# Band attention into a mixture of experts on one core: how w1 is prepared in the second pass, and three moved steps

## Chip, core and metric

One core of one Trainium2 chip runs the whole program. The metric is the device time of one execution in microseconds, the median over several runs. Times inside an execution come from the hardware profiler, counted from the span's start.

## What is computed

Attention over a band, then a mixture of experts on its result. Everything is float32.

```python
# q, k, v: (4, 8, 576, 64); window 32; heads 4 to 7 with dilation 4
scores = scale * q @ k.T, masked to the band
attn   = softmax(scores)
x      = (attn @ v) as (2304, 512)
# w1: (4, 512, 1024), w2: (4, 1024, 512), p: (2304, 4) from domain_probs
for e in range(4):
    out += p[:, e:e+1] * (relu(x @ w1[e]) @ w2[e])
```

## The kernel before

**Units and blocks.** The 4 experts are cut into 16 units of 256 hidden columns (u), the 2304 rows of x into 3 blocks of 768 (m). Each float32 operand is split into a high half, rounded to the type that TensorE multiplies (ScalarE's copy), and a low half, the rest (a subtraction on VectorE or GpSimd); a product is three matmuls. Most products are done by Strassen's scheme: seven products of quarter matrices in place of eight, with sums of quarters as operands. The operands of w1 are A11, A12, A22 and the sums S1 to S4 of its quarters, those of x B11, B21, B22 and T1 to T4, those of w2 the seven parts P1 to P7.

**First pass** (to about 277 us of the span). Units 0 to 11 meet block 0 while attention still runs. The generator `experts` yields one piece of TensorE work after another; the main loop takes one piece, calls `flush`, then lets the current round of attention (`pairs_of_steps`) go on by one yield, then a step of the queue of preparations. `split` makes a high half at once and puts the subtraction into `held` when something is holding; `flush` issues what is held. `mm1_b` is the second part of a unit's seven products: it asks for each part of x by `need_x` (which calls `need`, which calls `flush` first and last), multiplies, and lets VectorE add two results (s at L638, u at L643). In `mm1_b` "room" lets `room` make a preparation of x with the low half held. A round of attention ends with the copies `s_out` (ScalarE, L517) of the previous steps' output and with `s_norm` (GpSimd, L404) of the new ones. Each prepared w1 operand of units 2 to 11 is stored in HBM (`keep_w1`).

**Second pass** (from 277 us). 18 groups, each a pair of units on a block, in the order of `groups`. The loop over n runs the first products (`m1`, 14 pieces) of group n beside the second products (`m2`, P1, P5, P6, P3, P7, P2, P4) of group n-1; iteration n has seven steps b, each with two pieces of `m1`, one of `m2` and a call of `background(b)`. After every piece of `m1` the SP queue gets the load of that operand for the next unit (L833), which waits until TensorE has read the old one. In front of and behind the products stand ScalarE's copies out of PSUM (L884, L888, L890, L896) and its high halves (L904), VectorE's sums (L886, L892, L894, L932), low halves (L911, L916) and weighted sums into `acc` (L690).

`background(b)` issues two kinds of preparation. `w2_parts` makes the seven parts of w2 for the next pair: high half on ScalarE (L992), low half on GpSimd (L993), sums on GpSimd (L997, L1000, L1005, L1010). It starts when a new pair begins (`n in begins`: 2, 4, 6, 8, 10, 12, 13, 15, 17) with step 1 and goes on into the first two steps of the next iteration. `w1_again` does the same for w1 of units 12 to 15, 0 and 1, whose operands were not kept: it loads the rows of w1 into one tile (L1017), then for each of seven operands makes the sum if there is one (GpSimd, L1030), the high half (ScalarE, L1033) and the low half (GpSimd, L1034) into one tile `again`, and stores it (SP, L1036). Each of these is one call; `background` makes three calls a step, two where a pair begins, from iteration 1 on:

```python
            t = pools["late"].tile([128, 2, 2, 128], F32R, tag="again", name="again")
            nc.scalar.activation(out=t[:, 0], in_=src, func=AF.Copy)
            tt(out=t[:, 1], in0=src, in1=t[:, 0].bitcast(F32), op=ALU.subtract)
            yield
            nc.sync.dma_start(
...
                for _ in range(3 - (n in begins) if n else 0):
                    if again and next(again[0], 0) == 0:
                        again.pop(0)
```

All engines work through their own instructions in the order written here; a scheduler moves nothing.

Of the kernel before, what the change touches and what calls it, by code (L numbers as in the profile page):

```python
# [8 lines left out]
F32 = mybir.dt.float32  # L9
F32R = mybir.dt.float32r  # L10
# [38 lines left out]
def kernel(  # L49
# [231 lines left out]
    def attention(ap, xrp, pa, steps):  # L281
# [120 lines left out]
        def s_norm(n, gs):  # L402
            sm, rc = st[n]
            nc.gpsimd.tensor_tensor(  # L404
                out=sm, in0=sm, in1=rc.unsqueeze(2).to_broadcast([128, 2 * GS, KB]),
                op=ALU.mult,
            )
            st[n] = sm
# [93 lines left out]
        def s_out(n, gs, engines=None):  # L502
            po = st.pop(n)
            for k, (b, p, gi) in enumerate(gs):
                x = x_raw(b)[:, p, :]
                src = po[k][:, :GW]
                if p < NP // 2:
                    nt = GW // DILATION
                    dst = x.rearrange("q (r t) -> q r t", r=DILATION)
                    dst = dst[:, :, gi * nt:(gi + 1) * nt]  # L510
                    src = src.rearrange("q (t r) -> q r t", r=DILATION)
                else:
                    dst = x[:, gi * GW:(gi + 1) * GW]
                if engines and engines[k] == "v":
                    nc.vector.tensor_copy(out=dst, in_=src)
                else:
                    nc.scalar.activation(out=dst, in_=src, func=AF.Copy)  # L517
# [18 lines left out]
        def pairs_of_steps(new, old, begun, loaded):  # L536

            for m in old:
                s_tr(m, steps[m])
            if old:  # L540
                yield
            if new and not begun:
                for stage in (s_qk, s_max):
                    for m in new:
                        stage(m, steps[m])
                yield
            for stage in (s_sub, s_exp):
                for m in new:
                    stage(m, steps[m])
                    yield  # L550
            if not begun:
                loaded(len(new), 0)
                yield
            s_sums([(m, steps[m]) for m in new])
            for m in old:
                s_av(m, steps[m], True)
            for m in old[:1]:
                s_out(m, steps[m])
            yield
            for m in old[1:]:  # L560
                s_out(m, steps[m])
            if old:
                loaded(0, len(old))
                yield
            for m in new:
                s_norm(m, steps[m])
                yield

        return chunk, load_masks, load_qk, load_v, stages, at_first, pairs_of_steps

# [53 lines left out]
    def mm1_b(k):  # L624
        u, m = k
        x, u2, s5 = st.pop(k), tmp("u2"), tmp("s5")
        need_x(m, ("T2",))
        product(x, u, "S2", m, "T2", False)
        nc.scalar.activation(out=u2, in_=x, func=AF.Copy)
        yield "room"  # L630
        y = bank("x")
        need_x(m, ("T1",))
        product(y, u, "S1", m, "T1", True)
        nc.scalar.activation(out=s5, in_=y, func=AF.Copy)
        yield "room"
        need_x(m, ("T3",))
        product(x, u, "S3", m, "T3", False)
        nc.vector.tensor_tensor(out=s5, in0=x, in1=s5, op=ALU.add)  # L638
        yield
        need_x(m, ("B22",))  # L640
        product(y, u, "S4", m, "B22", False)
        h_hi(k, "22", s5)
        nc.vector.tensor_tensor(out=u2, in0=y, in1=u2, op=ALU.add)  # L643
        h_lo(k, "22", s5)
        h_out(k, "12", u2)
        yield "full"
        need_x(m, ("T4",))
        product(x, u, "A22", m, "T4", False)
        h_out(k, "21", x)
        yield "full"  # L650
# [364 lines left out]
    def w1_again(u, r):  # L1015

        nc.sync.dma_start(out=r, in_=w1_rows(u))  # L1017
        kept[u] = dram.tile([NO, 128, 2, FU], F32, name=f"w1_{u}")
        yield
        a11, a12 = r[:, 0:2, 0:128], r[:, 2:4, 0:128]  # L1020
        a21, a22 = r[:, 0:2, 128:256], r[:, 2:4, 128:256]
        tt = nc.gpsimd.tensor_tensor
        for n, src, one, two, op in (
            ("A11", a11, None, None, None), ("A12", a12, None, None, None),
            ("A22", a22, None, None, None), ("S1", a22, a21, a22, ALU.add),
            ("S3", a21, a11, a21, ALU.subtract), ("S2", a11, a22, a11, ALU.subtract),
            ("S4", a12, a12, a11, ALU.subtract),
        ):
            if op is not None:
                tt(out=src, in0=one, in1=two, op=op)  # L1030
                yield
            t = pools["late"].tile([128, 2, 2, 128], F32R, tag="again", name="again")
            nc.scalar.activation(out=t[:, 0], in_=src, func=AF.Copy)  # L1033
            tt(out=t[:, 1], in0=src, in1=t[:, 0].bitcast(F32), op=ALU.subtract)  # L1034
            yield
            nc.sync.dma_start(  # L1036
                out=kept[u][KEPT.index(n)].rearrange("p s f -> p (s f)"),
                in_=t.bitcast(F32).rearrange("p s c f -> p (s c f)"),
            )
            yield  # L1040

    def second_pass(tiles):

# [32 lines left out]
        for n in range(len(groups) + 1):  # L1076
# [18 lines left out]
                    first_over()  # L1095

            def background(b):
                if n == 0 and b < 5 or n and n in begins and b > 0 or n - 1 in begins and b < 2:
                    while w2_steps and next(w2_steps[0], 0) == 0:
                        w2_steps.pop(0)  # L1100
                if n + 1 in begins:
                    run = begins.index(n + 1)
                    if b in (2, 3):
                        spare = n in begins and (
                            raw_again.rearrange("p c f -> p (c f)").rearrange(
                                "p (c d) -> p c d", c=2
                            ), pools["other"],
                        )
                        if spare:
                            assert not again  # L1110
                        fetch_w2_half(runs2[run][0][b - 2], spare and spare[b - 2] or None)
                    elif b == 6:
                        w2_steps.append(w2_parts())
                for _ in range(3 - (n in begins) if n else 0):
                    if again and next(again[0], 0) == 0:
                        again.pop(0)
                if n == BACK + 1:
                    away_x(PRODUCTS[b][1], True)
                if n == BACK + 2 and b == 4:
                    acc_t[0] = acc_t[1]  # L1120
                    nc.sync.dma_start(
                        out=acc_t[0], in_=away["acc"].rearrange("a p d -> p a d")
                    )
# [540 lines left out]
```

## Time and profile before

| | us |
|---|---|
| median of 3 runs | 832.32 (830.87 to 834.38) |
| the profiled execution, its own time | 834.22 |
| span of the profiled execution | 832.2 |
| TensorE busy | 796.6 |
| VectorE busy | 611.0 |
| ScalarE busy | 361.5 |
| GpSimd busy | 406.6 |
| mean granted TensorE clock | 0.989 of full speed |

The span is the time from the first to the last instruction of one execution; the rest of its time lies around it. Busy time counts instructions at work, without waits. A wait is told as idle time of an engine just before an instruction, with what ended it.

### The profile page before, as it was taken

The numbers are of one execution on the slowest core, as the hardware profiler recorded it, in microseconds if no ns is written. First come the engines' busy times: TensorE is split into PE (matmuls) and PEld (weight loads), VectorE is DVE, ScalarE is ACT, GpSimd is POOL, SyncE is SP. The second block draws the span as 40 slices with busy tenths as digits, with TensorE's granted clock in tenths as the row PEclk, the third lists the DMA queues.
The fourth block names the chain that finished last, engine by engine and source line by source line (L and its number), as shares of the span: only waits on it lengthen the run. The fifth ranks groups of instructions, "written<-read, shape, count | busy, mean of one in ns | idle before, by whom it ended". The sixth has DMA issues, their size and how long they took to land.

```text
span 832.2 us, 18128 instructions
## 1 busy us (share of the span) xinstructions
PE 796.6 (96%) x6998; PEld 751.9 (90%) x6998; DVE 611.0 (73%) x1267; ACT 361.5 (43%) x723; POOL 406.6 (49%) x388
## 2 busy tenths in 40 slices
PE   7999999999999989899898999999999999999997
PEld 4778888888888879889898999999999999999997
DVE  6787666666686576667756687886977988788697
ACT  5455454544555344433533443443433454244341
POOL 5646796877696334725642661520511553052051
PEclk9999999999999999989998999999999999999998
DMA  8768668875668666465465566444454546965612
GB/s 243 213 185 246 217 214 258 287 264 188 215 218 280 203 212 202 152 203 184 158 208 171 155 201 212 125 147 151 124 171 125 178 127 221 380 226 176 214 38 77
DMA packets 108561, 161.60 MB, mean 194 GB/s; under 512 B 8873, under 2 KB 57513, under 8 KB 108475
## 3 DMA queue, kind: packets, MB, share of 16 engines
q1 hardware_dynamic: 107771, 159.88, 60.2%
q8 instruction: 56, 0.92, 0.5%
q10 hardware_dynamic: 704, 0.56, 0.2%
q14 instruction: 30, 0.25, 0.1%
HBM read 119.25 MB, written 41.16 MB: 193 GB/s over the span
## 4 chain that ended last, share of the span: by engine, by line
PE 71%; DVE 8%; POOL 6%; DMA 6%; ACT 5%; issue 3%; SPq 0%; DVEq 0%; POOLq 0%; ACTq 0%
PE m1x L577 21%; PE x L950 15%; PE m1y L577 11%; PE y L950 10%; PE m L709 10%; DMA w<-again 3%; DVE acc L690 2%; DMA r<-w 2%; POOL w_P L993 2%; PE po L435 2%; PE sc L346 1%; POOL again L1034 1%; DVE xr L257 1%; POOL sm L404 1%; DMA qk_s<-kT 1%
## 5 line engine op out<-in xcount | busy, mean ns | idle before, releaser
L993 POOL TENSOR_TENSOR w_P<-r,w_P 128x512 fp32r<-128x512 f32 x70 | 98.8, 1411 | 246.1 <-ACT w_P L992 127.5
L690 DVE SCALAR_TENSOR_TENSOR acc<-x,pn,acc 128x256 f32<-128x256 f32 x198 | 83.1, 473 | 8.8 <-PE x L950 8.7
L932 DVE SCALAR_TENSOR_TENSOR g<-g 128x768 f32<-128x768 f32 x72 | 88.6, 1230 | 0.6
L1034 POOL TENSOR_TENSOR again<-r,again 128x256 fp32r<-128x256 f32 x42 | 36.7, 874 | 87.5 <-ACT again L1033 87.5
L577 PE MATMUL m1x<-xh_B,s_A 128*128 128x384 f32 x288 | 74.0, 338 | 3.6 <-ACT g L884 3.6
L690 DVE SCALAR_TENSOR_TENSOR acc<-y,pn,acc 128x256 f32<-128x256 f32 x156 | 65.5, 473 | 11.2 <-PE y L950 10.7
L950 PE MATMUL y<-w_P,h0h 128*128 128x256 f32 x432 | 69.8, 284 | 1.5 <-ACT h0h L904 1.5
L950 PE MATMUL x<-w_P,xh_T 128*128 128x256 f32 x432 | 71.1, 288 | 0.0
L690 DVE SCALAR_TENSOR_TENSOR acc<-m,pn,acc 128x512 f32<-128x512 f32 x66 | 49.1, 748 | 29.5 <-PE m L709 29.5
L992 ACT ACTIVATE w_P<-r 128x512 fp32r<-128x512 f32 x70 | 43.9, 627 | 50.9 <-POOL r L1010 22.4
L950 PEld LDWEIGHTS y<-w_P,h0h 128*128 128x128 f32 x432 | 61.6, 191 | 2.1 <-ACT h0h L904 2.1
L950 PEld LDWEIGHTS x<-w_P,xh_T 128*128 128x128 f32 x432 | 63.1, 195 | 0.0
L577 PE MATMUL m1y<-xh_B,s_S 128*128 128x384 f32 x208 | 54.8, 345 | 7.4 <-ACT g L888 7.4
L577 PE MATMUL m1x<-xh_T,s_S 128*128 128x384 f32 x224 | 58.1, 341 | 3.0 <-ACT g L890 2.9
L709 PE MATMUL m<-w2h,hh 128*128 128x512 f32 x144 | 58.7, 408 | 1.2 <-DVE acc L690 1.1
L1033 ACT ACTIVATE again<-r 128x256 fp32r<-128x256 f32 x42 | 17.5, 416 | 96.9 <-DMA w<-again 57.9
L916 DVE TENSOR_TENSOR h0l<-g,h0h 128x768 fp32r<-128x768 f32 x36 | 38.6, 1072 | 25.9 <-ACT h0h L904 25.8
L709 PE MATMUL m<-w2l,hh 128*128 128x512 f32 x144 | 56.5, 393 | 0.0
L577 PEld LDWEIGHTS m1x<-xh_B,s_A 128*128 128x128 f32 x288 | 51.1, 188 | 4.5 <-ACT g L884 4.5
L904 ACT ACTIVATE h0h<-g 128x768 fp32r<-128x768 f32 x36 | 30.3, 841 | 56.7 <-DVE g L932 56.7
L911 DVE SCALAR_TENSOR_TENSOR h1l<-g,h1h 128x768 fp32r<-128x768 f32 x18 | 24.3, 1350 | 33.8 <-ACT h1h L904 33.8
L577 PE MATMUL m1x<-xl_B,s_A 128*128 128x384 f32 x144 | 48.4, 336 | 0.0
(215 smaller groups left out, 2274.9 us busy)
## 6 DMA issues: line engine op xcount, KB each, us to landing
s_S<-w SPq DMA_DIRECT2D x144, 256.0 KB, 2.8
s_A<-w SPq DMA_DIRECT2D x108, 256.0 KB, 2.8
r<-w SPq DMA_DIRECT2D x49, 512.0 KB, 4.1
w<-again SPq DMA_DIRECT2D x42, 256.0 KB, 2.0
v_s<-vw SPq DMA_DIRECT2D x48, 192.0 KB, 5.1
w<-g2h SPq DMA_DIRECT2D x10, 512.0 KB, 4.9
w<-g2l SPq DMA_DIRECT2D x10, 512.0 KB, 5.8
k_s<-kT SPq DMA_DIRECT2D x21, 224.0 KB, 5.2
```

The costliest lines, as they stand in the source:

```text
L577: nc.tensor.matmul(bank, w[:, k], x[:, k], start=(first and k == 0 and n == 0), stop=(last and k == 1 and n == len(parts) - 1), skip_group ...
L690: nc.vector.scalar_tensor_tensor(out=acc, in0=po, scalar=pn[:, tt, e:e + 1], in1=acc, op0=ALU.mult, op1=ALU.add,)
L709: nc.tensor.matmul(po, h, w, start=(n == 0 and x == 0), stop=(n == 3))
L904: nc.scalar.activation(out=h_places[n][0], in_=source(g, n), func=AF.Relu if n in RAW else AF.Copy)
L911: nc.vector.scalar_tensor_tensor(out=l, in0=source(g, n), scalar=0.0, in1=h.bitcast(F32), op0=ALU.max, op1=ALU.subtract,)
L916: nc.vector.tensor_tensor(out=l, in0=source(g, n), in1=h.bitcast(F32), op=ALU.subtract)
L932: nc.vector.scalar_tensor_tensor(out=g.h[n], in0=g.h[one], scalar=0.0, in1=g.h[two], op0=ALU.max, op1=op)
L950: nc.tensor.matmul(to, h_places[factor][low][:, c, t * 128:(t + 1) * 128], w[:, x, c], start=begins and k == 0 and t != 1, stop=k == len(o ...
L992: nc.scalar.activation(out=h, in_=src, func=AF.Copy)
L993: nc.gpsimd.tensor_tensor(out=l, in0=src, in1=h.bitcast(F32), op=ALU.subtract)
L1033: nc.scalar.activation(out=t[:, 0], in_=src, func=AF.Copy)
L1034: tt(out=t[:, 1], in0=src, in1=t[:, 0].bitcast(F32), op=ALU.subtract)
```

## The change

In `w1_again` the tile `again` gets two buffers; a call now stores the operand of the call before, makes the next high and low half and then the sum that the operand after it needs, so that a unit takes 10 calls (load, nothing, seven operands, last store) where it took 20. `background` makes one call a step from iteration 1 on. In `mm1_b` only the first visited unit asks for the parts of x. In a round of attention the first `s_norm` stands ahead of the rest of the copies and the second comes a yield later, so that a round has a yield less. And where a new pair begins and the next iteration begins another pair, or is the last (n = 12 and 17), w2's preparation starts with step 0.

```diff
@@ pairs_of_steps
             for m in old[:1]:
                 s_out(m, steps[m])
             yield
+            for m in new[:1]:
+                s_norm(m, steps[m])
             for m in old[1:]:
                 s_out(m, steps[m])
+            yield
+            for m in new[1:]:
+                s_norm(m, steps[m])
             if old:
                 loaded(0, len(old))
-                yield
-            for m in new:
-                s_norm(m, steps[m])
-                yield
+            yield
@@ mm1_b
-        need_x(m, ("T2",))
+
+        def ready(n):
+            if u == visits[0][0]:
+                need_x(m, (n,))
+
+        ready("T2")
...
@@ w1_again
         yield
+        yield
...
-        for n, src, one, two, op in (
-            ("A11", a11, None, None, None), ("A12", a12, None, None, None),
-            ("A22", a22, None, None, None), ("S1", a22, a21, a22, ALU.add),
-            ("S3", a21, a11, a21, ALU.subtract), ("S2", a11, a22, a11, ALU.subtract),
-            ("S4", a12, a12, a11, ALU.subtract),
-        ):
-            if op is not None:
-                tt(out=src, in0=one, in1=two, op=op)
-                yield
-            t = pools["late"].tile([128, 2, 2, 128], F32R, tag="again", name="again")
-            nc.scalar.activation(out=t[:, 0], in_=src, func=AF.Copy)
-            tt(out=t[:, 1], in0=src, in1=t[:, 0].bitcast(F32), op=ALU.subtract)
-            yield
+
+        def store(n, t):
             nc.sync.dma_start(
                 out=kept[u][KEPT.index(n)].rearrange("p s f -> p (s f)"),
                 in_=t.bitcast(F32).rearrange("p s c f -> p (s c f)"),
             )
+
+        ready = None
+        for n, src, following in (
+            ("A11", a11, None), ("A12", a12, None), ("A22", a22, (a22, a21, a22, ALU.add)),
+            ("S1", a22, (a21, a11, a21, ALU.subtract)),
+            ("S3", a21, (a11, a22, a11, ALU.subtract)),
+            ("S2", a11, (a12, a12, a11, ALU.subtract)), ("S4", a12, None),
+        ):
+            if ready:
+                store(*ready)
+            t = pools["late"].tile([128, 2, 2, 128], F32R, tag="again", name="again", bufs=2)
+            nc.scalar.activation(out=t[:, 0], in_=src, func=AF.Copy)
+            tt(out=t[:, 1], in0=src, in1=t[:, 0].bitcast(F32), op=ALU.subtract)
+            if following:
+                out_, one, two, op = following
+                tt(out=out_, in0=one, in1=two, op=op)
+            ready = n, t
             yield
+        store(*ready)
+        yield
@@ background
-                if n == 0 and b < 5 or n and n in begins and b > 0 or n - 1 in begins and b < 2:
+                alone = n in begins and n + 1 in (*begins, len(groups))
+                if n == 0 and b < 5 or n and n in begins and (alone or b > 0) or n - 1 in begins and b < 2:
...
-                for _ in range(3 - (n in begins) if n else 0):
-                    if again and next(again[0], 0) == 0:
-                        again.pop(0)
+                if n and again and next(again[0], 0) == 0:
+                    again.pop(0)
+                    next(again[0], 0) if again else None
```

Lines below `pairs_of_steps` move down by 2, those in and below `mm1_b` by 7, those below `w1_again` by 17.

The SP queue in iteration 1, where the first rows of w1 are loaded into r_4047. `w_12` is the kept w1 of unit 12, `s_...` are the operands of the next unit for the first products, `r<-w` the rows of w2. Before:

```order
L1017 DMA r_4047<-w 128x4x256
L1036 DMA w_12_4316<-again 128x512
L833 DMA s_S_3738<-w_3_1538 128x512
L833 DMA s_S_3737<-w_3_1538 128x512
L1036 DMA w_12_4316<-again 128x512
L833 DMA s_S_3740<-w_3_1538 128x512
L833 DMA s_S_3739<-w_3_1538 128x512
L975 DMA r<-w 128x2x512
L1036 DMA w_12_4316<-again 128x512
```

With the change:

```order
L1024 DMA r_4047<-w 128x4x256
L840 DMA s_S_3738<-w_3_1539 128x512
L840 DMA s_S_3737<-w_3_1539 128x512
L840 DMA s_S_3740<-w_3_1539 128x512
L840 DMA s_S_3739<-w_3_1539 128x512
L982 DMA r<-w 128x2x512
L840 DMA s_A_3736<-w_4_1865 128x512
L840 DMA s_A_4045<-w_3_1539 128x512
L982 DMA r<-w 128x2x512
L1033 DMA w_12_4316<-again 128x512
```

The first store moved from directly behind the row load to three steps behind it.

ScalarE at the turn from iteration 17 to the drain, where the last parts of w2 are made (w_P_4194 is P7, w_P_4311 is P2, w_P_4365 and in the change w_P_4361 is P4). Before:

```order
L992 ACTIVATE w_P_4194<-r 128x512
L904 ACTIVATE h0h<-g 128x768
L896 ACTIVATE g<-m1x 128x384
L992 ACTIVATE w_P_4311<-r 128x512
L992 ACTIVATE w_P_4365<-r 128x512
L904 ACTIVATE h1h<-g 128x768
```

With the change:

```order
L999 ACTIVATE w_P_4311<-r 128x512
L911 ACTIVATE h0h<-g 128x768
L903 ACTIVATE g<-m1x 128x384
L999 ACTIVATE w_P_4361<-r 128x512
L911 ACTIVATE h1h<-g 128x768
```

P2 and P4 moved ahead by a step each; P4 no longer stands directly behind P2.

VectorE in a unit's second part in the first pass, at the sum s of L638; `xl_B_1` are low halves of block 1's x. Before:

```order
L139 TENSOR_TENSOR xl_B_1_1836<-xr,xh_B_1_1835 128x2x192
L139 TENSOR_TENSOR xl_B_1_1891<-xr,xh_B_1_1890 128x2x192
L638 TENSOR_TENSOR s_3063<-m1y,s_3063 128x384
L643 TENSOR_TENSOR u_3062<-m1x,u_3062 128x384
L602 SCALAR_TENSOR_TENSOR hl<-s_3063,hh 128x384
```

With the change:

```order
L139 TENSOR_TENSOR xl_B_1_1838<-xr,xh_B_1_1837 128x2x192
L645 TENSOR_TENSOR s_3064<-m1y,s_3064 128x384
L139 TENSOR_TENSOR xl_B_1_1891<-xr,xh_B_1_1890 128x2x192
L650 TENSOR_TENSOR u_3063<-m1x,u_3063 128x384
L604 SCALAR_TENSOR_TENSOR hl<-s_3064,hh 128x384
```

The second subtraction moved from ahead of the sum s to behind it, ahead of the sum u.

## Rows read from the trace of the kernel before

**Rows 1.** The page, part 1: busy time and share of the span.

```profile
PE 796.6 (96%) x6998; PEld 751.9 (90%) x6998; DVE 611.0 (73%) x1267; ACT 361.5 (43%) x723; POOL 406.6 (49%) x388
```

**Rows 2.** Windows: stretch, length, busy us of each engine (instructions), granted clock, DMA.

```profile
276.84:513.29 236.45, 219.08 (x1471) 213.01 (x1471) 159.11 (x268) 95.52 (x177) 113.49 (x102) 0.97 0.58 189
414.62:451.67 37.05, 33.28 (x211) 32.24 (x211) 23.00 (x40) 12.82 (x25) 13.40 (x14) 0.91 0.58 192
451.67:483.00 31.33, 30.49 (x212) 29.76 (x211) 21.82 (x38) 14.65 (x27) 19.99 (x16) 1.00 0.51 163
513.29:542.99 29.70, 29.70 (x212) 29.70 (x211) 24.64 (x38) 13.23 (x22) 12.10 (x8) 1.00 0.45 125
542.99:572.69 29.70, 29.70 (x211) 29.70 (x211) 23.44 (x40) 10.71 (x18) 4.50 (x3) 1.00 0.51 159
513.29:780.56 267.27, 267.27 (x1891) 267.27 (x1891) 218.82 (x343) 109.51 (x179) 83.20 (x55) 1.00 0.58 182
809.47:832.20 22.73, 17.39 (x126) 16.77 (x126) 16.59 (x29) 4.71 (x8) 4.51 (x3) 0.90 0.21 70
```

**Rows 3.** Waits: engine line <- waited for: us in total, times, longest.

```profile
ACT again L1033 <- DMA w<-again: 57.9, 25, 7.0
...
ACT again L1033 <- DMA r<-w: 24.6, 6, 7.2
...
ACT again L1033 <- POOL r L1030: 14.4, 5, 4.1
...
PE m1y L577 <- DVE s L638: 3.1, 4, 1.0
```

**Rows 4.** Groups by line, ScalarE, 513.29 to 780.56 us (busy, mean | idle before).

```profile
L992 ACT ACTIVATE w_P<-r 128x512 fp32r<-128x512 f32 x35 | 22.0, 628 | 29.1 <-POOL r L1010 14.4 <-POOL r L997 13.2 <-POOL r L1005 1.5
```

**Rows 5.** Timeline, ScalarE and TensorE: start, length, instruction [idle before <- releaser].

```profile
364.72 0.42 ACT L1033 ACTIVATE again<-r 128x256 fp32r<-128x256 f32 x1 [6.97 <-DMA w<-again]
365.04 0.47 ACT L884 ACTIVATE g<-m1x 128x384 f32<-128x384 f32 x1
...
365.56 0.64 PE L577 MATMUL m1x<-xh_B,s_A 128*128 128x384 f32 x2 [1.84 <-ACT g L884]
```

**Rows 6.** DMA issues: count, KB each, median us from issue to landing.

```profile
w<-again SPq DMA_DIRECT2D x42, 256.0 KB, 2.0
```

**Rows 7.** Chain that ended last, second pass: start, length, what.

```profile
298.12 4.34 DMA w<-again
...
432.60 7.39 DMA r<-w
```

**Rows 8.** Groups by line, GpSimd, from 277 us on.

```profile
L993 POOL TENSOR_TENSOR w_P<-r,w_P 128x512 fp32r<-128x512 f32 x65 | 92.3, 1420 | 240.4 <-ACT w_P L992 124.7 <-PE m1y L577 65.7 <-DMA s_A<-w 32.8
L1034 POOL TENSOR_TENSOR again<-r,again 128x256 fp32r<-128x256 f32 x42 | 36.7, 874 | 87.5 <-ACT again L1033 87.5
L1030 POOL TENSOR_TENSOR r<-r 128x256 f32<-128x256 f32 x24 | 22.8, 948 | 0.3
L997 POOL TENSOR_TENSOR r<-r 128x512 f32<-128x512 f32 x9 | 16.4, 1821 | 0.7
```

**Rows 9.** Timeline of the drain behind iteration 17, VectorE, ScalarE and TensorE.

```profile
810.59 2.05 DVE L932 SCALAR_TENSOR_TENSOR g<-g 128x768 f32<-128x768 f32 x1
...
813.83 0.63 ACT L992 ACTIVATE w_P<-r 128x512 fp32r<-128x512 f32 x1 [3.43 <-POOL r L1010]
...
815.25 0.74 PE L950 MATMUL x<-w_P,h1h 128*128 128x256 f32 x4 [1.20 <-ACT h1h L904]
...
816.55 0.95 DVE L932 SCALAR_TENSOR_TENSOR g<-g 128x768 f32<-128x768 f32 x1
816.68 0.51 PE L950 MATMUL x<-w_P,h1l 128*128 128x256 f32 x2 [0.69 <-DVE h1l L916]
```

**Rows 10.** Timeline in a unit's second part of the first pass, VectorE and TensorE.

```profile
178.74 0.79 DVE L139 TENSOR_TENSOR xl_B<-xr,xh_B 128x384 fp32r<-128x384 f32 x1 [0.72 <-ACT xh_B L142]
...
180.05 0.45 PE L577 MATMUL m1y<-xh_T,g1h 128*128 128x384 f32 x1 [1.03 <-DVE s L638]
```

More of the change, by code (lines that the diff above doesn't have):

```diff
@@ L631, in mm1_b @@
         y = bank("x")
-        need_x(m, ("T1",))
+        ready("T1")
         product(y, u, "S1", m, "T1", True)
@@ L635, in mm1_b @@
         yield "room"
-        need_x(m, ("T3",))
+        ready("T3")
         product(x, u, "S3", m, "T3", False)
@@ L639, in mm1_b @@
         yield
-        need_x(m, ("B22",))
+        ready("B22")
         product(y, u, "S4", m, "B22", False)
@@ L646, in mm1_b @@
         yield "full"
-        need_x(m, ("T4",))
+        ready("T4")
         product(x, u, "A22", m, "T4", False)
```

## Prediction

> **What bounds the kernel now.** Read the page's busy shares first: TensorE is busy 96% of the span [rows 1], so a change can win only where TensorE stands still or runs at a lower clock, and the question is where those places are. The windows view, cut at the first matmul of P1 in each step of the second pass's pipeline, gives them [rows 2]. I call such a stretch an iteration; iteration n computes the first products of group n beside the second products of group n-1. From 513.29 us on nine iterations take 267.27 us, 29.70 each, with TensorE busy for all of it, whether ScalarE and GpSimd prepare w2 beside it (12.10 us of GpSimd work in iteration 8) or next to nothing (4.50 in iteration 9). That is TensorE's own time. The seven iterations before it take 236.45 us, where 7 x 29.70 would be 207.90: **28.55 us too much**. Of these TensorE is idle 236.45 - 219.08 = 17.4 us; the mean granted clock of 0.97 is about 7 us (two iterations, the one shown among them, stand at 0.91, that is, part of them at 1.2 instead of 2.4 GHz); the rest is in matmuls that run longer around a stall.
>
> The waits view says who stands ahead of TensorE there. The copies of L1033, the first half of a prepared w1 operand, stop ScalarE for 57.9 us behind the store of the one buffer `again`, 24.6 us behind the row load, and 14.4 us behind a GpSimd sum [rows 3]. ScalarE works its queue in order, so what stands behind such a copy is late. The timeline shows one case [rows 5]: the copy waits 6.97 us for the store; the copy of L884 behind it empties a bank late; TensorE waits 1.84 us. TensorE's waits in these iterations go back to a late ScalarE in this way; in the nine iterations from 513.29 on ScalarE still waits 29.1 us ahead of 35 copies of w2 [rows 4] and TensorE never, so ScalarE can lose some 0.8 us at such a place at no cost.
>
> **The change, part by part.**
>
> *w1 in the second pass.* Before, one call did a copy with its subtraction, a sum, or a store, and two or three calls followed each other in one seventh of an iteration (a step, 29.70 / 7 = 4.24 us): copy, store and next copy were one chain through ScalarE, GpSimd, the SP queue and HBM. Now a step has one call. The store of a half leaves in the step after its copy, and its buffer is wanted again only a step later still; the sum is made in the step before the copy that reads it; the row load has two steps. The work is the same (42 copies, 42 subtractions, 24 sums, 42 stores), spread over iterations 1 to 9 instead of 1 to 7: 10 calls a unit, 60 in all, 7 an iteration.
>
> Does each wait fit? A store lands in 2.0 us at the median [rows 6]; the longest in the chain took 4.34 [rows 7]. SP sends it at the end of the step after the copy, behind that step's two loads, and the buffer is next written a step later: 4.24 us, plus what ScalarE may be late. Covered. The longest row load in the chain took 7.39 [rows 7]; two steps are 8.5 us. Covered, just. On SP the store goes out a step after GpSimd's subtraction and no longer stops there for it, so the loads behind it move up too.
>
> What is late next is GpSimd. In a step with w2 it has one subtraction of 1.42 us, mostly a sum of 1.82, one w1 subtraction of 0.87 and often a w1 sum of 0.95 [rows 8]: 5.06 us at worst against 4.24, but 1.42 + 0.87 = 2.29 where neither sum falls. Over an iteration it is 7 x 1.42 + 4 x 1.82 + 4.9 x 0.87 + 2.8 x 0.95 = 24.1 of 29.7 us, for 7 of 10 calls make a subtraction and 4 of 10 a sum. So it catches up. The cost that stays I bound by 0 (iteration 8, w2 alone) and by what iteration 6 loses today with as much w1 work and all waits in it, 31.33 - 29.70 = 1.6 us [rows 2]; for the four iterations with w2 (2, 4, 6, 8) that is 0 to 6.5 us. I take 2.0, nearer to iteration 8, because the store and load waits leave. **Term: -28.55 + 2.0 = -26.5 us**, ends -22 and -28.5.
>
> *w2 a step earlier in the last two single groups.* In iteration 17 the preparation now starts in the first step, so nothing of it is left for the drain. There today ScalarE waits 3.43 us for GpSimd's last sum, the operand h1h behind it is late, TensorE waits 1.20 and 0.69 us [rows 9], and then 3.41 us go at half clock (most of the 0.90 of that window [rows 2]), which costs 1.7. All of it would be 3.6 us. But without first products between them the second products follow each other faster than VectorE's chain of sum, subtraction and sum, so I leave about half: **-2.0 us**, ends 0 and -3.6. The new write of a w2 place now follows right behind the product that read it; ScalarE waits for that product (some 2 us) in iterations 12, 13 and 17, and what stands behind it, h1h, is wanted only by the next product but one. Cost 0; without that slack 1 us each.
>
> *Block 0's x asked for once.* The removed requests asked for nothing new; they only flushed held subtractions. VectorE then does the sum s (L638) ahead of the second held `xl`, no longer behind it. TensorE waited for that sum four times, 3.1 us in all [rows 3]; the case shown has an `xl` of 0.79 us just ahead of the sum and a wait of 1.03 behind it [rows 10]. What is late next is the sum u, which frees the other bank; the six matmuls of A22 lie ahead of its reader. **-2.5 us**, ends -4 and +1 (an `xl` of 0.79 that lands on u instead).
>
> *Norms ahead of copies.* GpSimd gets its multiplication a yield earlier, ScalarE one copy later; rounds lose a yield, and TensorE's order shifts by a piece of six matmuls here and there. The same matmuls run. I cost it at 0, ends -1 and +1; the cover is TensorE's own queue of first-pass products.
>
> **Sum:** -26.5 - 2.0 - 2.5 = -31.0 us. The profiled execution took 834.22 us, so 803.2; it lies 1.9 above the median of the runs shown, 832.32, and 801.5 is what I expect of a median.
>
> **Rivals.**
>
> *GpSimd becomes the bound in the w2 iterations.* If every step with both sums costs its 0.8 us over, four steps in each of four iterations, 13 us come back: 801.5 + 11 = 812.5 beyond the 2.0 already counted. For it: the means above. Against it: these sums rarely meet, and iteration 6 loses 1.6 today with the same load. The means hold contention: L932 on VectorE takes 2.05 us beside GpSimd's sum and 0.95 without [rows 9]. The Trainium skill, GPSIMD Engine Reference, section Key points, says that GpSimd shares its SBUF interfaces with VectorE and contends with VectorE instructions that have two SBUF inputs; L932 is one, and the trace agrees. Chance 0.13.
>
> *The store wait stays.* If the copies still wait for a store each, only the waits for load and sum go, 39.0 of 96.9 us of ScalarE's waiting, 40% of 28.55 = 11.5 us: 832.3 - 11.5 - 4.5 = 816. Against it: the order on SP, where a copy's store now has a step's loads ahead of it and another copy behind. Chance 0.06.
>
> *Slower.* Its place is the SP queue. Each store leaves only after a step's two loads, which wait for TensorE. If it lands later than a step plus ScalarE's slack, 4.24 + 0.8 = 5.0 us, each of the 42 copies is late by the difference, where today 36 waits cost 28.55 us together. It breaks even with what the change wins (28.55 + 4.5) at 0.8 us a copy, a landing of 5.8; at 6.5 us the copies lose 42 x 1.5 = 63 us, and 832 - 33 + 63 = 862 would come out. Against it: the median of 2.0 [rows 6]. Chance 0.02.
>
> *No effect* (ScalarE's waits were not what held TensorE): 832. Against it stands the timeline [rows 5]. Chance 0.03.
>
> **Numbers.** Forecast 0.76, GpSimd 0.13, store wait 0.06, none 0.03, slower 0.02. The forecast's own terms reach from 834.2 - 36 to 834.2 - 21 in the profiled execution, 796 to 811 in a median; that range holds most of the first case, and the GpSimd rival begins at its upper end. A measurement of this kernel can tell about 0.5% from no change, 4 us: faster 0.94, same 0.03, slower 0.03.
>
> **What would show it.** Iterations 1 to 9 at 29.7 to 30.3 us each with a granted clock of 1.00; the copies of `again` waiting for stores and row loads for under 15 us together (82.5 now); no L638 among TensorE's waits; the drain after iteration 17 about 2 us shorter. It is wrong if iterations 2, 4, 6 and 8 stand well above the odd ones with ScalarE waiting for GpSimd's sums (the first rival), or if `again` still waits for stores.

## The result and the profile after

The changed kernel takes **802.12 us** at the median of four runs (801.16 to 802.85); the kernel before, measured beside it, 833.35 (830.87 to 835.88). The ratio is 0.9624, with a 95% interval of 0.9591 to 0.9657. The forecast was 801.5, in a range of 796 to 811.

The page, part 1, answers to [rows 1]: the busy time of VectorE, ScalarE and GpSimd is what it was or a little more, the span is 33.0 us shorter, and TensorE has lost 12.5 us of busy time (in a stretch at half clock, and around a stall, matmuls count as busy for longer: iteration 5 of the kernel before counted 33.28 us at a clock of 0.91 and its iteration 6 30.49 at 1.00, where an undisturbed one counts 29.70 [rows 2]).

```profile
span 799.2 us, 18123 instructions
...
PE 784.1 (98%) x6998; PEld 745.2 (93%) x6998; DVE 615.0 (77%) x1267; ACT 361.8 (45%) x723; POOL 412.4 (52%) x388
```

The windows view, cut as in [rows 2]: iterations 1 to 7 together, iterations 5, 6 and 8, iterations 9 to 17, the drain.

```profile
273.68:481.98 208.30, 208.18 (x1472) 207.86 (x1472) 165.76 (x267) 94.47 (x170) 107.94 (x90) 1.00 0.63 200
392.48:422.58 30.10, 29.98 (x212) 29.66 (x212) 22.66 (x40) 12.44 (x23) 9.45 (x10) 1.00 0.65 210
422.58:452.27 29.69, 29.69 (x211) 29.69 (x211) 24.01 (x38) 14.45 (x26) 21.17 (x17) 1.00 0.62 195
481.98:511.67 29.69, 29.69 (x211) 29.69 (x211) 24.84 (x39) 13.89 (x25) 18.17 (x13) 1.00 0.58 178
...
511.67:778.44 266.77, 266.37 (x1886) 266.05 (x1885) 215.66 (x342) 110.63 (x184) 92.74 (x64) 1.00 0.57 182
778.44:799.20 20.76, 16.01 (x126) 15.31 (x126) 15.92 (x29) 4.20 (x7) 1.34 (x1) 0.95 0.23 77
```

So the 33.0 us come from four places: iterations 1 to 7 give 236.45 - 208.30 = **28.15**, the start of iteration 1 lies 276.84 - 273.68 = 3.16 earlier, the drain is 22.73 - 20.76 = 1.97 shorter, and of the rest (iterations 8 to 17) 0.3 is lost, in iteration 17. Every one of iterations 1 to 9 now stands at 29.69 to 29.71 with TensorE busy throughout, but for iteration 5, at 30.10. Iteration 6 holds GpSimd for 21.17 of its 29.69 us, and TensorE does not notice.

The waits of the second pass answer to [rows 3] (who waits <- for what: us in total, times, longest):

```profile
POOL again L1049 <- ACT again L1048: 47.1, 20, 6.0
...
ACT again L1048 <- DMA w<-again: 13.5, 11, 2.2
...
ACT again L1048 <- POOL r L1052: 9.2, 9, 2.0
...
PEld m1y L579 <- ACT g L895: 0.4, 1, 0.4
```

ScalarE's copies wait for their stores 13.5 us where it was 57.9, for sums 9.2 where it was 14.4, and for the row load not at all where it was 24.6. Of ScalarE's work one wait of TensorE is left in the second pass: a weight load (PEld) stands 0.4 us behind the copy of L895, in iteration 5. The stores themselves did not become faster. The view of the tile `again` and of its stores says the contrary ([rows 6] had a median of 2.0):

```profile
L1049 POOL TENSOR_TENSOR again<-r,again x42: 733/751/1603, 283.6 to 523.5; 128x256 fp32r<-128x256 f32 x42
...
DMA to landing us min/median/max: 2.1/3.2/4.9
```

A store now lands in 3.2 us at the median, 4.9 at most, and is waited for less than a quarter as long, since its buffer is wanted only a step later.

The one loss left is at the turn to iteration 5. The timeline of ScalarE there (start, length, instruction [idle before <- releaser]):

```profile
389.67 0.42 ACT L1048 ACTIVATE again<-r 128x256 fp32r<-128x256 f32 x1 [1.48 <-POOL r L1052]
...
394.59 0.42 ACT L1048 ACTIVATE again<-r 128x256 fp32r<-128x256 f32 x1 [1.95 <-POOL r L1052]
...
397.20 0.64 ACT L999 ACTIVATE w_P<-r 128x512 fp32r<-128x512 f32 x1 [1.81 <-POOL r L1017]
398.60 0.42 ACT L1048 ACTIVATE again<-r 128x256 fp32r<-128x256 f32 x1 [0.76 <-POOL r L1052]
```

Here the sums of w1 (L1052) meet the last sums of w2 (L1017) on GpSimd, and ScalarE waits four times in 10 us; the copy of L895 stands behind the last of these, and TensorE loses 0.4. This is the cost for which the forecast set aside 2.0.

### The profile page after: what moved, and what is told of

Its sections match the earlier page's. It is cut to its first block, busy times and chain, and to the rows that moved or that the text cites. A ratio compares the mean times of both kernels' runs of the same rounds, so it can differ in the third digit from the quotient of the medians.

```text
span 799.2 us, 18123 instructions
## 1 busy us (share of the span) xinstructions
PE 784.1 (98%) x6998; PEld 745.2 (93%) x6998; DVE 615.0 (77%) x1267; ACT 361.8 (45%) x723; POOL 412.4 (52%) x388
## 4 chain that ended last, share of the span: by engine, by line
PE 87%; DVE 7%; POOL 2%; ACT 2%; issue 1%; DVEq 0%; POOLq 0%; ACTq 0%
PE m1x L579 27%; PE x L957 18%; PE m1y L579 14%; PE y L957 14%; PE m L716 10%; PE po L435 2%; DVE acc L697 1%; DVE xr L257 1%; PE sc L346 1%; DVE sm L360 1%; PE pt L415 1%; POOL sm L404 1%; DVE hl L604 1%; DVE xl_B L139 0%; DVE su L391 0%
## 5 line engine op out<-in xcount | busy, mean ns | idle before, releaser
L1000 POOL TENSOR_TENSOR w_P<-r,w_P 128x512 fp32r<-128x512 f32 x70 | 95.3, 1361 | 234.1 <-ACT w_P L999 146.3
L939 DVE SCALAR_TENSOR_TENSOR g<-g 128x768 f32<-128x768 f32 x72 | 92.5, 1285 | 0.6
L1049 POOL TENSOR_TENSOR again<-r,again 128x256 fp32r<-128x256 f32 x42 | 41.7, 993 | 60.7 <-ACT again L1048 47.1
L957 PE MATMUL x<-w_P,xh_T 128*128 128x256 f32 x432 | 69.2, 282 | 0.0
L911 ACT ACTIVATE h0h<-g 128x768 fp32r<-128x768 f32 x36 | 30.3, 843 | 69.0 <-DVE g L939 69.0
L957 PEld LDWEIGHTS x<-w_P,xh_T 128*128 128x128 f32 x432 | 61.1, 189 | 0.0
L923 DVE TENSOR_TENSOR h0l<-g,h0h 128x768 fp32r<-128x768 f32 x36 | 38.2, 1061 | 22.9 <-ACT h0h L911 22.9
L579 PE MATMUL m1y<-xh_B,s_S 128*128 128x384 f32 x208 | 53.2, 337 | 0.1
L716 PE MATMUL m<-w2h,hl 128*128 128x512 f32 x144 | 45.2, 393 | 0.0
L895 ACT ACTIVATE g<-m1y 128x384 f32<-128x384 f32 x36 | 17.6, 489 | 60.3 <-PE m1y L579 60.3
```

The costliest lines, as they stand in the source:

```text
L579: nc.tensor.matmul(bank, w[:, k], x[:, k], start=(first and k == 0 and n == 0), stop=(last and k == 1 and n == len(parts) - 1), skip_group ...
L716: nc.tensor.matmul(po, h, w, start=(n == 0 and x == 0), stop=(n == 3))
L895: copy(out=g.h[v, 1][:, 1], in_=to, func=AF.Copy)
L911: nc.scalar.activation(out=h_places[n][0], in_=source(g, n), func=AF.Relu if n in RAW else AF.Copy)
L923: nc.vector.tensor_tensor(out=l, in0=source(g, n), in1=h.bitcast(F32), op=ALU.subtract)
L939: nc.vector.scalar_tensor_tensor(out=g.h[n], in0=g.h[one], scalar=0.0, in1=g.h[two], op0=ALU.max, op1=op)
```

## The experiments

Three theories were put to the test. **Distance** (mine): a copy must not follow in the same step on the store and the sum that it needs; two buffers and one call a step together give that. **Capacity** (the first rival): GpSimd's amount of work in an iteration decides. **Buffer alone**: the second buffer does it all, the new rhythm nothing. Mine took this sharp form only with the run of two calls a step, which I had expected otherwise. Ratios are to the kernel before on the same chip; the "loss" of an iteration is its length less 29.70 us.

### The w1 part alone

The kernel before with the new `w1_again` and with one call a step:

```diff
-                for _ in range(3 - (n in begins) if n else 0):
-                    if again and next(again[0], 0) == 0:
-                        again.pop(0)
+                if n and again and next(again[0], 0) == 0:
+                    again.pop(0)
+                    next(again[0], 0) if again else None
```

> The kernel before with the change's w1_again and its one call a step, nothing else. By the prediction's first term the second pass's iterations 1 to 7 lose their excess: 28 us less, 804 to 806, the drain unchanged and the first products of the second pass as late as before. If a good part of the whole gain came from the other edits, or if the parts need each other, it stays above 808.

Measured: 806.52 us against 834.87, ratio 0.9661 (0.9633 to 0.9689). Iterations 1 to 9 stand at 29.7 us with one of 30.08, the drain at 22.51. The time is half a microsecond above what I expected. This part is worth 28.35 of the 31 us; the rest lies in the other edits.

### Buffers and rhythm apart

The kernel before with two buffers and nothing else:

```diff
-            t = pools["late"].tile([128, 2, 2, 128], F32R, tag="again", name="again")
+            t = pools["late"].tile([128, 2, 2, 128], F32R, tag="again", name="again", bufs=2)
```

> The kernel before with two buffers for the tile again and nothing else: copy, sum and store are still single calls, two or three a step. If the store was what held ScalarE (theory of the prediction), ScalarE's waits for stores fall from 57.9 to under 15 us, those for row loads and sums stay, and some 60% of 28.5 us goes: 813 to 820. If it is the number of calls in a step that matters (rival), ScalarE waits for the sums and loads in the stores' place and the time stays above 826.

Measured, as expected: 818.07 us, ratio 0.9802 (0.9764 to 0.9840). Waits of ScalarE in it:

```profile
ACT again L1033 <- POOL r L1030: 23.6, 12, 4.1
ACT again L1033 <- DMA r<-w: 21.0, 5, 6.4
ACT again L1033 <- DMA w<-again: 5.7, 5, 1.8
```

The store wait is nearly gone, even more than with the whole change (13.5), yet iterations 1 to 7 still lose 11.2 us of the 28.55: load and sum still stop the copies. The buffer alone is worth 17.4 us, some 60%.

The other way round, the change with one buffer:

```diff
-            t = pools["late"].tile([128, 2, 2, 128], F32R, tag="again", name="again", bufs=2)
+            t = pools["late"].tile([128, 2, 2, 128], F32R, tag="again", name="again")
```

> The changed kernel with one buffer: a call stores the half of the call before and then copies into the same tile. If the buffer matters, every copy but the first waits for the store sent just before it, 2 to 4 us each, iterations 1 to 9 stand at 31 to 34 us and the time is 815 to 830. If the slower pace alone did it (rival), iterations stay under 30.3 us and the time is 802 to 806.

Measured, as expected: 826.19 us (823.78 to 828.61), ratio 0.9900 (0.9850 to 0.9949). The waits of ScalarE and the window of iterations 1 to 9:

```profile
ACT again L1048 <- DMA w<-again: 104.2, 35, 6.7
```

```profile
274.63:568.82 294.19, 276.96 (x1891) 271.12 (x1891) 213.59 (x344) 118.92 (x216) 128.28 (x113) 0.98 0.58 180
```

Nine iterations lose 294.19 - 267.3 = 26.9 us. With one buffer the rhythm gives the second pass only 1.7 us in this execution: load and sum are no longer waited for (but for one sum of w2, 2.8 us), the store all the more. The profiled execution is the slower of the two, which lie 4.8 apart; by the medians the one buffer costs 24.1 us of the change, so the rhythm alone gives some 4 of the 28.35 of the w1 part. Buffer and rhythm need each other: "buffer alone" falls with the run before, and the rhythm alone with this one.

### Two calls a step

The change, with the same calls at twice the pace:

```diff
-                if n and again and next(again[0], 0) == 0:
-                    again.pop(0)
-                    next(again[0], 0) if again else None
+                for _ in range(2 if n else 0):
+                    if again and next(again[0], 0) == 0:
+                        again.pop(0)
+                        next(again[0], 0) if again else None
```

> The changed kernel with two calls of w1_again a step in place of one: w1 is done by iteration 5, with two copies, two subtractions and up to two sums of GpSimd a step. If GpSimd's time in a step decides (the first rival of the prediction: 5.06 us for one call beside w2, 6.9 for two), iterations 2 and 4 lose 2 us or more each, ScalarE waits for sums, 808 to 820. If ScalarE's slack takes it up, 802 to 805.

Measured: 836.54 us, ratio 1.0008 (0.9976 to 1.0039): everything is given back, far beyond what I expected. The windows of iterations 1 to 5 in it, and ScalarE's waits:

```profile
275.98:310.93 34.95, 31.32 (x212) 31.00 (x211) 22.96 (x39) 13.19 (x25) 13.38 (x14) 0.95 0.69 226
310.93:345.07 34.14, 30.73 (x212) 29.69 (x212) 25.26 (x38) 14.48 (x29) 25.76 (x23) 1.00 0.57 186
345.07:386.59 41.52, 34.49 (x212) 33.49 (x212) 24.55 (x41) 16.08 (x31) 20.19 (x22) 0.88 0.60 209
386.59:421.14 34.55, 30.97 (x211) 29.67 (x211) 22.50 (x37) 14.16 (x28) 21.32 (x19) 1.00 0.56 183
421.14:458.61 37.47, 32.18 (x212) 31.66 (x211) 25.08 (x41) 14.38 (x27) 12.53 (x14) 0.91 0.57 183
```

```profile
ACT again L1048 <- POOL r L1052: 33.5, 16, 4.5
ACT again L1048 <- DMA w<-again: 22.9, 9, 5.6
ACT again L1048 <- DMA r<-w: 11.4, 5, 3.3
```

Capacity would put the loss where GpSimd has most to do. Iteration 2, with 25.76 us of GpSimd work, loses 4.4 us; iteration 3, with 20.19, loses 11.8, and iteration 1, with 13.38, 5.2. (Part of what iterations 1, 3 and 5 lose more is the clock, 0.88 to 0.95; but by TensorE's idle time alone, 3.6, 3.4, 7.0, 3.6 and 5.3 us, the loss does not follow GpSimd's work either.) Nor is GpSimd without rest for long: in these iterations it never works for more than 8.6 us without a gap of at least 0.12 us. That leaves the distance: with two calls in a step, the sum, the copy that reads it, and the store and the copy that overwrites its buffer come within one step of each other again. The chain of waits shows one such place, in iteration 1 (start, length, what):

```profile
288.22 0.42 SPq L982
...
288.74 6.01 DMA w<-again
...
294.85 0.42 ACT again L1048
295.27 0.39 ACT g L891
...
295.70 2.29 PE m1x L579 x6
```

The store left SP behind a row load of w2, took 6.01 us, the copy waited for it, the copy out of PSUM (L891) stood behind that copy, and TensorE waited 3.63 us. That is the mechanism of the "slower" rival. At this pace it takes its part, but the copies wait longer for sums (33.5 us) than for stores (22.9).

### The sum a step ahead

The change, with each sum moved back into the call of the copy that reads it, ahead of that copy:

```diff
+            if before:
+                out_, one, two, op = before
+                tt(out=out_, in0=one, in1=two, op=op)
             if ready:
                 store(*ready)
...
             tt(out=t[:, 1], in0=src, in1=t[:, 0].bitcast(F32), op=ALU.subtract)
-            if following:
-                out_, one, two, op = following
-                tt(out=out_, in0=one, in1=two, op=op)
```

> The changed kernel with each sum moved back into the call that copies it, ahead of the copy; two buffers, one call a step and stores as in the change. With two calls a step all of the gain was lost, and more in iterations 1, 3 and 5 than in 2 and 4, which speaks for a chain within a step rather than for GpSimd's time. If a copy that waits for a sum of its own step is what costs (chain theory), iterations with w2 (2, 4, 6, 8), where GpSimd reaches the sum late, lose 1 to 3 us each and the others stay at 29.7 to 30: 805 to 814. If the sum's place is of no account, 801 to 803.

Measured: 814.61 us, ratio 0.9766 (0.9699 to 0.9833), 0.6 above what I expected; 12.4 us are lost in iterations 1 to 9, nearly all in 2, 4, 5, 6 and 9 (1.6, 2.0, 2.8, 3.8 and 2.1). That 5 and 9 lose and 8 does not is not the pattern that I expected; w2's preparation does reach into the first steps of 5 and 9, but into those of 3 and 7 as well, so which iterations lose stays open. ScalarE's waits:

```profile
ACT again L1051 <- POOL r L1047: 34.9, 12, 4.2
ACT again L1051 <- DMA w<-again: 13.5, 10, 2.3
```

The store wait is that of the change to the tenth; the sum wait went from 9.2 to 34.9. GpSimd does the same work, each sum a step later, and its longest stretch without such a gap is 8.2 us in these iterations; so the place of the sum alone is worth 12 us.

### How near GpSimd is

The change, with each subtraction of w1 made twice (the second repeats the first):

```diff
             tt(out=t[:, 1], in0=src, in1=t[:, 0].bitcast(F32), op=ALU.subtract)
+            tt(out=t[:, 1], in0=src, in1=t[:, 0].bitcast(F32), op=ALU.subtract)
```

> The changed kernel with every one of the 42 subtractions of w1_again on GpSimd issued twice: 1 us more of GpSimd a step, the chain within a step as it was. If GpSimd's time in a w2 step decides (the prediction's first rival), the w2 steps go from 5 to 6 us and iterations 2, 4, 6 and 8 lose 3 us or more each: 812 to 820. If there is room, as 24 of 29.7 us say, GpSimd catches up, iterations lose under 1 us each: 802 to 806.

Measured: 811.15 us, ratio 0.9725 (0.9657 to 0.9792), between what the two theories expected; 8.1 us are lost in iterations 1 to 9. Windows of iterations 2 and 5, and the timeline of GpSimd from iteration 4 on, and of ScalarE and TensorE in iteration 5:

```profile
305.53:335.22 29.69, 29.69 (x211) 29.69 (x211) 23.13 (x39) 13.86 (x25) 22.25 (x18) 1.00 0.59 178
395.38:428.72 33.34, 29.96 (x211) 29.64 (x211) 24.58 (x40) 14.04 (x26) 15.36 (x16) 1.00 0.62 205
```

```profile
373.65 1.29 POOL L1000 TENSOR_TENSOR w_P<-r,w_P 128x512 fp32r<-128x512 f32 x1 [14.25 <-ACT w_P L999]
...
404.01 0.72 POOL L1053 TENSOR_TENSOR r<-r 128x256 f32<-128x256 f32 x1
...
404.76 0.42 ACT L1048 ACTIVATE again<-r 128x256 fp32r<-128x256 f32 x1 [1.54 <-POOL r L1053]
405.09 0.83 ACT L911 ACTIVATE h1h<-g 128x768 fp32r<-128x768 f32 x1
405.82 0.47 ACT L895 ACTIVATE g<-m1y 128x384 f32<-128x384 f32 x1
...
406.34 0.61 PE L579 MATMUL m1y<-xh_B,s_S 128*128 128x384 f32 x2 [3.38 <-ACT g L895]
```

Iteration 2 loses nothing with 22.25 us on GpSimd, iteration 5 loses 3.6 with 15.36. But a cut at the iterations hides what happens at the turn: from 373.65, in iteration 4, to 408.06, in iteration 5, GpSimd works for 34.4 us without a gap of more than 0.1 us, and what it is behind with from iteration 4 is what the copies of iteration 5 wait for. In the change the longest such stretch is 16.3 us (384.24 to 400.52), at the same turn. So GpSimd can become the bound, by its work over the stretch in which it has no rest and not by its total in an iteration: the first rival's mechanism is real, and 0.7 to 1.4 us more a step (the length of the added instruction, 1.06 on average) brings it out. Capacity explains this run; it does not explain the two before it, where GpSimd has gaps all along.

### The second step of the row load

The change without the empty call behind the load:

```diff
         yield
-        yield
         a11, a12 = r[:, 0:2, 0:128], r[:, 2:4, 0:128]
```

> The changed kernel without the added empty call: the row load has one step (4.24 us) instead of two. A load lands in 4.2 us at the median, so ScalarE waits for most of the six loads, 1 to 3 us each, 5 to 15 us in all, and TensorE loses 1 to 5 us: 803 to 807. If ScalarE's slack takes that up, 801 to 803 and no wait of TensorE behind L1048.

Measured: 802.77 us, ratio 0.9624 (0.9559 to 0.9690), the same as the change. The copies wait for the row load again, but twice, 3.8 us in all, and ScalarE's slack takes it. I had expected a small loss; the load does not need its second step.

### The drain and the first pass

The kernel before, with w2 a step earlier in the single groups (the line of `alone`) and nothing else:

> The kernel before with w2's preparation begun a step earlier in iterations 12 and 17, nothing else. By the prediction the drain after iteration 17 (22.7 us) is 2 us shorter (0 to 3.6), the waits behind h1h of 1.20 and 0.69 us mostly gone, iterations 12, 13 and 17 stay at 29.7. If the earlier write behind its reader costs ScalarE what the drain wins (rival), iteration 12, 13 or 17 is 1 us longer and the whole is unchanged.

Measured: 831.84 us against 834.24, ratio 0.9976 (0.9949 to 1.0003), not to be told from none by the time alone; in the profile the drain is 20.44 us, 2.3 shorter than before, and iteration 17 takes 29.19 for 28.91.

The kernel before with both edits of the first pass, then with each alone (`ready` in `mm1_b`; `s_norm` ahead of the copies in `pairs_of_steps`):

> The kernel before with the first-pass edits alone (x asked for once, norms ahead of copies). The prediction's term is 2.5 us: the second pass starts 2 to 4 us earlier than 276.8 and the time is about 830, the sum s gone from TensorE's waits but for one. If the gain seen in the whole change's first pass was chance between runs, it starts within 1 us of 276.8.

> The kernel before with block 0's x asked for once, nothing else. By the prediction TensorE's waits for the sum s fall from 3.1 to about 0 us and the second pass starts 2.5 us earlier than 276.8. If the low halves only move their delay onto the sum u (rival), a wait for u of 1 us or more takes its place and the start is within 1 us.

> The kernel before with the norms ahead of the copies, nothing else. Costed at 0 (within 1 us): the second pass starts between 275.8 and 277.8. If the earlier norms free the next round's transposes (rival), it starts 1.5 us earlier or more and TensorE's wait for the norm (L404) is gone.

Measured: both 830.99 us against 834.87 (0.9956, 0.9942 to 0.9970); x asked for once 830.34 against 834.24 (0.9936, 0.9910 to 0.9963); norms alone 833.28 (0.9984, 0.9958 to 1.0009). To see the first pass by itself I take the stretch from TensorE's wait of 1.1 us for `acc` (L690 before, at 74.57 us) to the start of iteration 1; what lies ahead of it varies between executions, as the last section tells. It is 202.27 us before, 200.34 with both, 199.54 with x asked for once, 200.79 with the norms alone, and 200.25 in the change. The norms kernel did win 1.5 us there, but its iteration 1 took 39.0 us where before it took 35.8. The stretch repeats well: it is 202.27 to 202.97 (202.6 on average) in the four kernels here with the first pass of the kernel before, and 200.03 to 200.34 (200.2) in the seven with that of the change.

The change without the norms, to see what they add beside the rest:

> The changed kernel with the norms behind the copies again, as before. Alone, asking once won 2.7 us from TensorE's wait at 75 us to the second pass, the norms 1.5, both together 2.0: if that holds, this stretch is 199.5 us against 200.2 of the changed kernel, and the time 800.5 to 802.5, perhaps 0.7 us better than the change. If the norms add to the other edit, the stretch is 201 or longer.

Measured: 801.64 us (800.98 to 802.34), ratio 0.9608 (0.9557 to 0.9659), not to be told from the change; the stretch is 199.89. TensorE's waits in that stretch, first in the change, then without the norms:

```profile
PE m1y L579 <- DVE s L645: 0.9, 1, 0.9
PE m1x L579 <- DVE u L650: 0.6, 1, 0.6
PE m L716 <- ACT hh L598: 0.4, 1, 0.4
```

```profile
PE pt L415 <- POOL sm L404: 0.4, 1, 0.4
PE sc L346 <- ACT pts L419: 0.2, 1, 0.2
```

Asking once takes the four waits for s away for good; the norms take away the 0.4 us for L404 and bring waits of 0.9, 0.6 and 0.4 on VectorE and ScalarE in its place.

## Why the prediction was right, and where its steps were not

The median came within 0.6 us of the forecast, 802.12 against 801.5. Part of that is luck: between the two profiled executions the time fell by 33.1 us, where the sum said 31.0, because w1 gave 1.65 more than its term and the start of iteration 1 0.7 more; the profiled execution of the kernel before lay 0.9 above its median, that of the change 1.0 below.

- **w1: right.** -26.5 was forecast with ends of -22 and -28.5; measured -28.15, and the w1 part alone moved the median by -28.35. The mechanism is the one named: two buffers without the rhythm, the rhythm without two buffers, and both at twice the pace each bring waits and a loss of TensorE back, the first a part of it.
- **The cost that stays of GpSimd: mis-sized.** I took 2.0 us, spread over the iterations with w2. It is 0.4, in iteration 5, where no new w2 begins. The 24.1 us of GpSimd work that I reckoned for an iteration with w2 were 18.2 to 21.2. My price came from iteration 6 of the kernel before, which lost 1.6. TensorE's longest wait there (0.42 us) was for h0h, and h0h stood behind a copy of w1 that had waited 3.46 us for a sum (rows below); GpSimd made that sum just ahead of the copy, behind two operations of w2, and had stood idle for 3.48 us before these. So that was the sum's place and not GpSimd's amount of work, for in the change the same iteration loses nothing with 21.17 us of GpSimd. The fitting row was iteration 8, the other bound.
- **"Covered, just" for the row load:** covered with room, since one step serves as well.
- **Store: right.** 4.24 us plus ScalarE's slack against a landing that I read at 2.0 to 4.34; it became 2.1 to 4.9, below the 5.0 from which the slower rival would have begun, though not by much, and at two calls a step 6.01 was seen. "Covered" was not quite so: 11 of the 42 copies still wait for a store, 13.5 us in all and up to 2.2, and ScalarE's slack takes that.
- **Drain: right sum, wrong share.** -2.0 forecast, -1.97 measured. But I charged 1.7 us to the half clock [rows 2]. Four kernels with the drain as it was, in which it ran at a clock of 0.96 to 1.00, took 22.30 to 22.53 us where before took 22.73: the half clock cost some 0.2 to 0.4, as TensorE was idle longer in these (6.0 to 6.1 us against 5.3). The gain is the wait for h1h and what followed it. ScalarE's h1h now waits for VectorE's g alone (the row at 781.64 below). The move was not quite free: iteration 17 lost 0.3.
- **x asked for once: right,** -2.5 forecast, -2.7 in its stretch when alone (-3.1 against the average of the four old ones, and 3.9 by the medians, so rather more than forecast). **Norms at 0: right as the change stands,** though alone they win 1.5 in that stretch; the two do not add up, and together they give -2.0 (-2.4 between the averages). Beside the other edit the norms cost some 0.3: 199.89 without them. The sign that I named, no L638 (now L645) among TensorE's waits, is wrong: one of 0.9 stayed, and it goes when the norms go. The remaining 1.1 of the 3.16 us lies ahead of that stretch, where executions of the same code differ by more.
- **The rivals.** No effect and the store wait fell with the profile. That GpSimd becomes the bound fell here, but its margin is thin: some 1 us more a step brings it out.

Iteration 6 of the kernel before, ScalarE and TensorE:

```profile
463.77 0.42 ACT L1033 ACTIVATE again<-r 128x256 fp32r<-128x256 f32 x1 [3.46 <-POOL r L1030]
464.10 0.83 ACT L904 ACTIVATE h0h<-g 128x768 fp32r<-128x768 f32 x1
...
464.98 0.74 PE L950 MATMUL y<-w_P,h0h 128*128 128x256 f32 x4 [0.42 <-ACT h0h L904]
```

GpSimd's w1 instructions did get longer, while its w2 subtractions (L1000) got a little shorter. The groups of the second pass in the change ([rows 8] had 874, 948 and 1420 ns) and, in the drain, the sums of L939 on VectorE, the first beside GpSimd's L1000 (from 779.45 to 780.79), the second with GpSimd idle:

```profile
L1000 POOL TENSOR_TENSOR w_P<-r,w_P 128x512 fp32r<-128x512 f32 x65 | 88.8, 1366 | 228.4 <-ACT w_P L999 142.7 <-PE m1y L579 71.9 <-PE m1x L579 13.5
L1049 POOL TENSOR_TENSOR again<-r,again 128x256 fp32r<-128x256 f32 x42 | 41.7, 993 | 60.7 <-ACT again L1048 47.1 <-DMA s_A<-w 13.6
L1052 POOL TENSOR_TENSOR r<-r 128x256 f32<-128x256 f32 x24 | 25.8, 1074 | 0.5
```

```profile
779.56 2.04 DVE L939 SCALAR_TENSOR_TENSOR g<-g 128x768 f32<-128x768 f32 x1
...
781.64 0.84 ACT L911 ACTIVATE h1h<-g 128x768 fp32r<-128x768 f32 x1 [2.27 <-DVE g L939]
...
783.57 0.94 DVE L939 SCALAR_TENSOR_TENSOR g<-g 128x768 f32<-128x768 f32 x1
```

The w1 operations on GpSimd are 13% longer on average, the w2 subtractions 4% shorter. The timelines show where the 13% come from: 25 of the 66 w1 operations take 1.3 to 1.6 us (14 in the kernel before take 1.2 or more), and each of these began while VectorE was in the midst of an instruction that reads two operands from SBUF (L918, L923 or L939, in the kernel before L911, L916 or L932); the other 41 take 0.73 to 0.89. (The 2.05 us of L932 in [rows 9], which I read as beside a sum of GpSimd, began beside a subtraction, L993, 810.48 to 811.83.) The Trainium skill, GPSIMD Engine Reference, section Key points, says that GpSimd shares its SBUF interfaces with VectorE and contends with VectorE instructions that have two SBUF inputs. The trace agrees, in both directions: 2.04 against 0.94 us on VectorE, and on GpSimd the 25 operations just named, up to 1603 ns where 733 is the least for one and the same form.

## What to carry to other kernels

When an engine that works its queue in order feeds the bound engine, look at its waits by what it stands behind, and put producer, copy and store of a side job a whole step apart, with one buffer more than that distance; a second buffer without the distance gave 60% here, the distance without the buffer 2 to 4 of 28 us. Slow the side job down to a pace that fits its time: the same calls at twice the pace gave the whole gain back. And do not judge a helper engine by its total in a stage: it stalled others here by what stood ahead of the one instruction that was waited for, and by its amount of work only where it had gone 34 us without a gap.

## What the runs showed of the hardware

- A transfer can get slower and matter less: stores of 256 KB went from a median of 2.0 to 3.2 us, and cost less than before. With two buffers in the old rhythm the median was 2.2, with one buffer in the new 3.0, so it goes with the new rhythm, in which a store leaves SP behind a step's loads; which transfers slow it is not shown.
- The sum of ScalarE's waits is no measure of the loss: 104.2 us of waiting in 35 pieces cost TensorE 26.9 us, 22.7 us in 20 pieces 0.4, though single waits in the latter were up to 2.2 us.
- Executions of the same code differ in the first pass: in seven kernels whose first pass is that of the change, iteration 1 begins at 273.68 to 276.24 us (275.3 on average), in four with that of the kernel before at 276.70 to 277.58 (277.2). The averages stand 1.9 us apart, where those of the stretch stand 2.4 apart; the 3.16 of the two profiles compared above is partly luck.
